# A 16-float tile between two buffers: x, gh and gl 64 bytes further up in SBUF

## The chip, the cores and the metric

The kernel runs on one core of a Trainium2 chip. The metric is the device time of one execution in microseconds; for the kernel before it is 677.24 us, the median of three runs (676.77 to 677.29).

## The reference

Attention over 4 batches, 8 heads, 768 positions and head dimension 64, in which a query sees the first 4 keys (sinks) and the last 128, then a two-layer network over the 3072 tokens with a leaky rectifier between the layers:

```python
keep = is_sink | in_window
scores = np.where(keep, scale * (q @ k.T), -1e9)
a = softmax(scores)
x = (a @ v)                      # 3072 tokens x 512
h = x @ w_in                     # 512 -> 2048
g = np.maximum(h, 0.0) + alpha * np.minimum(h, 0.0)
out = (g @ w_out).astype(np.float32)   # 2048 -> 512
```

## The kernel before

The tokens go in 12 chunks of 256 (`NCHUNK`), the 2048 hidden units in 16 blocks of 128 (`NF`). Everything of a chunk is kept in halves: a value is split into a part rounded to the TensorE's fp32r format and the rest, so x is `xh` and `xl`, the hidden activations are `gh` and `gl`, and each weight block `w0` to `w15` holds four rows of 512 floats in each partition: high and low part of w_in, high and low part of w_out.

For a chunk c and a block f there is one **pair** of products. `gemm1` (line 894) makes 12 matmuls of 256 columns: for each of 4 slices of the 512 inputs, high weights with `xh`, high weights with `xl`, low weights with `xh`. The weight slice (128x128) is loaded into the array, `xh` or `xl` streams past it. `gemm2` (lines 931, 932 and 929) makes 6 matmuls of 512 columns with the roles exchanged: a 128x128 half of `gh` or `gl` is loaded into the array, and a row of the weight block streams past. Between the two, ScalarE and VectorE make `g`, `gh` and `gl` out of the PSUM bank (lines 898 to 901). There are 12 x 16 = 192 pairs; gemm2 of a block follows gemm1 of the block two places later (`LAG`).

Attention of the next chunk (scores at lines 597 and 598, softmax at 610 and 614, values at 786 and 875) is fed in between the pairs. The order on each engine comes out of `Plan`, a scheduler that draws a schedule from estimated costs and then ties the instructions of each engine into that order. No address enters its costs.

Two SBUF pools matter here. `const` holds the constants and the 16 weight blocks and lies at the low addresses. `main` lies behind it; its tiles are laid one behind the other in the order of the `several(...)` and `pool.tile(...)` calls, so every tile's address follows from the sizes ahead of it. Worked out from the built program, per partition and modulo 512 bytes:

| tile | start modulo 512, before | role at TensorE |
|---|---|---|
| w0 to w13, w15 | 32 | loaded in gemm1, streamed in gemm2 |
| w14 | 192 | the same |
| xh, xl (2 each) | 224 | streamed in gemm1 |
| gh, gl (3 each) | 224 | loaded in gemm2 |
| kq0, kq1 | 96, 128 | both, in the scores |
| sinkT, vs | 224, 224 | streamed, loaded, in the sinks' product (line 859) |

All slices that one matmul takes of x, gh, gl or a weight block begin a multiple of 512 bytes into the tile, so the remainder modulo 512 is the same for all of them. In gemm1 the streamed operand thus lies 192 bytes beyond the loaded one modulo 512 (32 bytes for block 14); in gemm2 the loaded one lies 192 bytes beyond the streamed one (32 for block 14).

Of the kernel before, what the change touches and what calls it, by code (L numbers as in the profile page):

```python
# [9 lines left out]
F32 = mybir.dt.float32  # L10
# [9 lines left out]
P = 128  # L20
# [301 lines left out]
def program(ctx, tc, qk, pairs, vp, vq, vs, w, par, out):  # L322
# [3 lines left out]
    pool = fast.enter_context(tc.tile_pool(name="main", bufs=1))  # L326
# [8 lines left out]
    def several(name, n, shape, dtype):  # L335
        plan.kind(name, [pool.tile(shape, dtype, name=f"{name}{i}") for i in range(n)])
# [17 lines left out]
    several("sinkT", 1, [P, QC], F32R)  # L354
    several("vs", 1, [P, DM], F32R)
    several("ob", 2, [P, DM], F32)
    several("xh", 2, [P, KT, QC], F32R)
    several("xl", 2, [P, KT, QC], F32R)
    several("g", 2, [P, QC], F32)
# [918 lines left out]
```

## Time and profile before

| what | us |
|---|---|
| median of the runs shown | 677.24 |
| runs shown | 676.77, 677.24, 677.29 |
| span of the profiled execution, first to last instruction | 676.2 |
| median less that span: what lies around it | 1.0 |
| VectorE busy in the span | 525.8 |
| ScalarE busy in the span | 397.5 |

The profile comes from one execution, of which the page gives the span and no other time. Matmuls are pipelined: the record of one reaches over the start of the next, so the distance from start to start, not the length of the records, says what a matmul costs in a stream.

### The profile page before, as it was taken

What the parts mean: (1) busy time and instruction counts of PE and PEld (TensorE: products, weight loads), DVE (VectorE), ACT (ScalarE), POOL (GpSimd) and SP (SyncE); (2) the same over time, 40 slices, a digit from 0 to 9 for tenths busy, and PEclk for the clock granted to TensorE, in tenths of its full rate; (3) what the DMA queues carried; (4) which work ended last, traced back from release to release, by engine and by line L of the source; (5) the groups of instructions that cost most, each with busy time, mean ns of one, the idle gap of its engine ahead of it and who ended that gap; (6) DMA issues with size and microseconds to landing.
All of it is one profiled execution on the core that took longest, in us unless ns stands there. A gap on an engine that the chain in (4) does not pass through costs nothing.

```text
span 676.2 us, 13243 instructions
## 1 busy us (share of the span) xinstructions
PE 663.8 (98%) x4532; PEld 580.5 (86%) x4534; DVE 525.8 (78%) x1750; ACT 397.5 (59%) x1066; POOL 34.5 (5%) x115
## 2 busy tenths in 40 slices
PE   9989999999999999999999999999999999999996
PEld 4577898888989989989988988988998988998995
DVE  6999999968967976986986995995895994994331
ACT  6989888827636726736636735644744753853332
POOL 2110000001000000000000000010000000000000
PEclk9979999999999999999999999999999999999999
DMA  8684641424343453443443433552542543420001
GB/s 314 229 277 151 241 187 39 127 71 147 122 133 107 122 148 93 145 132 95 141 118 114 143 107 93 163 140 61 172 128 78 161 128 88 142 94 17 32 2 35
DMA packets 58683, 85.19 MB, mean 126 GB/s; under 512 B 9072, under 2 KB 35056, under 8 KB 58608
## 3 DMA queue, kind: packets, MB, share of 16 engines
q1 hardware_dynamic: 55056, 71.17, 34.7%
q10 hardware_dynamic: 3552, 13.11, 5.4%
q8 instruction: 37, 0.61, 0.4%
q14 instruction: 38, 0.31, 0.1%
HBM read 67.22 MB, written 17.04 MB: 125 GB/s over the span
## 4 chain that ended last, share of the span: by engine, by line
PE 83%; DVE 9%; ACT 5%; issue 2%; POOL 0%; DMA 0%; ACTq 0%; SPq 0%; POOLq 0%
PE bank L894 35%; PE bank L931 12%; PE bank L932 11%; PE bank L929 11%; PE bank L786 3%; PE bank L598 3%; PE bank L597 3%; PE bank L875 2%; DVE wa L396 2%; ACT pt L614 1%; ACT wa L382 1%; DVE wa L394 1%; DVE w L404 1%; DVE g L899 1%; DVE gl L901 1%
## 5 line engine op out<-in xcount | busy, mean ns | idle before, releaser
L894 PE MATMUL bank<-xh,w 128*128 128x256 f32 x1536 | 307.9, 283 | 0.4 <-DVE g L899 0.2
L894 PEld LDWEIGHTS bank<-xh,w 128*128 128x128 f32 x1536 | 250.6, 189 | 9.0 <-DVE g L899 3.0
L894 PE MATMUL bank<-xl,w 128*128 128x256 f32 x768 | 215.1, 280 | 0.1
L898 ACT ACTIVATE g<-bank,param 128x256 f32<-128x256 f32 x192 | 90.5, 472 | 117.4 <-PE bank L894 113.1
L931 PE MATMUL bank<-w,gh 128*128 128x512 f32 x382 | 151.7, 397 | 0.2 <-ACT gh L900 0.2
L932 PE MATMUL bank<-w,gh 128*128 128x512 f32 x382 | 150.1, 393 | 0.0
L894 PEld LDWEIGHTS bank<-xl,w 128*128 128x128 f32 x768 | 145.2, 189 | 4.4 <-DVE xl L808 0.3
L614 ACT ACTIVATE pt<-pt,nm 128x260 f32<-128x260 f32 (+1 forms) x192 | 94.5, 493 | 53.5 <-DVE nm L610 53.1
L899 DVE TENSOR_TENSOR g<-bank,g 128x256 f32<-128x256 f32 x192 | 79.7, 419 | 51.4 <-ACT g L898 50.9
L929 PE MATMUL bank<-w,gl 128*128 128x512 f32 x382 | 119.5, 394 | 0.0
L900 ACT CAST gh<-g 128x256 fp32r<-128x256 f32 x192 | 76.9, 404 | 59.7 <-DVE g L899 59.6
L901 DVE TENSOR_TENSOR gl<-g,gh 128x256 fp32r<-128x256 f32 x192 | 80.5, 423 | 26.5 <-ACT gh L900 23.0
L610 DVE CUSTOM_DVE_ANT_0 pt<-bank,masks 128x260 f32<-128x260 f32 (+1 forms) x192 | 75.0, 401 | 19.3 <-PE bank L598 15.5
L929 PEld LDWEIGHTS bank<-w,gl 128*128 128x128 f32 x382 | 70.7, 188 | 16.2 <-issue 0.7
L931 PEld LDWEIGHTS bank<-w,gh 128*128 128x128 f32 x382 | 71.9, 188 | 9.5 <-ACT gh L900 0.7
L932 PEld LDWEIGHTS bank<-w,gh 128*128 128x128 f32 x382 | 71.9, 188 | 8.3
L563 DVE TENSOR_TENSOR kq<-stage,kq 64x392 fp32r<-64x392 f32 x80 | 45.3, 566 | 2.7
L659 POOL TENSOR_TENSOR sink<-pt,ri 128x8 f32<-128x8 f32 x80 | 20.8, 264 | 504.7 <-DVE ri L644 358.8
L597 PE MATMUL bank<-kq 128*128 128x260 f32 (+1 forms) x160 | 44.4, 278 | 1.3 <-DVE nm L610 1.3
L598 PE MATMUL bank<-kq 128*128 128x260 f32 (+1 forms) x160 | 45.0, 281 | 0.0
L655 DVE CUSTOM_DVE_ANT_0 comb<-pt,ri 128x128 f32<-128x128 f32 x136 | 43.1, 343 | 0.4
L561 ACT CAST kq<-stage 128x392 fp32r<-128x392 f32 x80 | 40.9, 512 | 0.7 <-ACT pt L614 0.2
(130 smaller groups left out, 686.9 us busy)
## 6 DMA issues: line engine op xcount, KB each, us to landing
stage<-qk SPq DMA_DIRECT2D x80, 324.0 KB, 2.9
wraw<-w ACTq DMA_DIRECT2D x12, 1024.0 KB, 5.9
swap<-comb SPq DMA_DIRECT2D x36, 256.0 KB, 2.0
comb<-swap SPq DMA_DIRECT2D x36, 256.0 KB, 3.2
v<-vq SPq DMA_DIRECT2D x36, 192.0 KB, 2.5
out_dram<-ob SPq DMA_DIRECT2D x22, 256.0 KB, 3.5
wraw<-w SPq DMA_DIRECT2D x4, 1024.0 KB, 12.0
v<-vp SPq DMA_DIRECT2D x8, 192.0 KB, 6.9
```

What stands on the lines that cost most here:

```text
L597: nc.tensor.matmul(s[:, w0], qh()[:, qs], ks()[:, kw], start=True, stop=False)
L598: nc.tensor.matmul(s[:, w0], ql()[:, qs], ks()[:, kw], start=False, stop=True)
L610: op("DVE", dve(n), lambda: nc.vector.tensor_tensor_reduce(out=pt.at[:, u, w0], in0=s.at[:, w0], in1=masks[:, i, w0], scale=-0.125, scalar ...
L614: op("ACT", exp(n), lambda: nc.scalar.activation(pt.at[:, u, w0], pt.at[:, u, w0], AF.Exp, bias=nm.at[:, h, u:u + 1], scale=-1.0, accum_ou ...
L894: nc.tensor.matmul(h(), fin.at[:, 0, part, ks], rhs.at[:, kt], start=(kt == 0 and n == 0), stop=(kt == KT - 1 and n == 2))
L898: op("ACT", act(QC, True), lambda: nc.scalar.activation(g.at, h(), AF.Copy, scale=alt[:, f:f + 1]), reads=[bk, known("param")], writes=[g])
L899: op("DVE", dve(QC), lambda: nc.vector.tensor_tensor(g.at, h(), g.at, ALU.max), reads=[bk], writes=[g])
L900: op("ACT", cast(QC), lambda: nc.scalar.copy(gh.at, g.at), reads=[g], writes=[gh])
L901: op("DVE", dve(QC), lambda: nc.vector.tensor_tensor(gl.at, g.at, gh.at.bitcast(F32), ALU.subtract), reads=[g, gh], writes=[gl])
L929: nc.tensor.matmul(o2[j].at, gl.at[:, js], fin.at[:, 1, 0], start=False, stop=(f == NF - 1))
L931: nc.tensor.matmul(o2[j].at, gh.at[:, js], fin.at[:, 1, 0], start=(f == 0), stop=False)
L932: nc.tensor.matmul(o2[j].at, gh.at[:, js], fin.at[:, 1, 1], start=False, stop=False)
```

## The change

One tile of 16 floats (64 bytes in each partition) is asked of the pool `main` behind `ob` and ahead of `xh`. Nothing writes or reads it.

```diff
     several("vs", 1, [P, DM], F32R)
     several("ob", 2, [P, DM], F32)
+    pool.tile([P, 16], F32, name="between")
     several("xh", 2, [P, KT, QC], F32R)
     several("xl", 2, [P, KT, QC], F32R)
     several("g", 2, [P, QC], F32)
     several("gh", LAG + 1, [P, QC], F32R)
     several("gl", LAG + 1, [P, QC], F32R)
```

Every tile of `main` behind it moves up by 64 bytes: xh, xl, g, gh, gl from 224 to 288 modulo 512, and the small tiles pf, wrap, masks and tri with them. All tiles ahead of it and all of `const` stay. The instructions of every engine, their order, their waits and their shapes are the same in both programs; only these addresses differ. In gemm1 the streamed x now lies 256 bytes beyond the loaded weights modulo 512 (96 for block 14), and in gemm2 the loaded gh and gl lie 256 beyond the streamed weights (96 for block 14).

## The prediction

> **What bounds the kernel now.** I read the page's busy times and clock first, then busy times by stretch, then who waited, and last the starts of single matmuls in the timeline.
>
> ```profile
> span 676.2 us, 13243 instructions
> PE 663.8 (98%) x4532; PEld 580.5 (86%) x4534; DVE 525.8 (78%) x1750; ACT 397.5 (59%) x1066; POOL 34.5 (5%) x115
> PEclk9979999999999999999999999999999999999999
> ...
> 28.00:100.00 72.00, 69.09 (x452) 57.86 (x451) 69.62 (x128) 62.31 (x131) 4.00 (x8) 0.95 0.62 214
> 100.00:300.00 200.00, 198.40 (x1361) 176.72 (x1359) 167.19 (x594) 119.75 (x337) 11.57 (x34) 1.00 0.38 114
> 300.00:600.00 300.00, 299.82 (x2107) 269.85 (x2107) 237.83 (x867) 170.31 (x489) 12.96 (x48) 1.00 0.41 121
> ...
> PE bank L588 <- DVE nm L610: 1.7, 2, 1.2
> PE bank L597 <- DVE nm L610: 1.3, 3, 0.8
> ```
>
> TensorE is busy 98% of the span at a granted clock of nine tenths or more in 39 of 40 slices, and its longest waits on another engine sum to 1.7 and 1.3 us. From 100 to 600 us it is busy 498.2 of 500 us, with VectorE at 405: a nanosecond taken off or put on a matmul there shows at the end almost whole. From 28 to 100 us VectorE is as full (69.62 of 72 us), so a faster TensorE would gain little there.
>
> The work that the change touches is nearly all of TensorE's:
>
> ```profile
> L894 PE MATMUL bank<-xh,w 128*128 128x256 f32 x1536 | 307.9, 283 | 0.4 <-DVE g L899 0.2
> L894 PE MATMUL bank<-xl,w 128*128 128x256 f32 x768 | 215.1, 280 | 0.1
> ...
> L931 PE MATMUL bank<-w,gh 128*128 128x512 f32 x382 | 151.7, 397 | 0.2 <-ACT gh L900 0.2
> L932 PE MATMUL bank<-w,gh 128*128 128x512 f32 x382 | 150.1, 393 | 0.0
> ...
> L929 PE MATMUL bank<-w,gl 128*128 128x512 f32 x382 | 119.5, 394 | 0.0
> ```
>
> 1536 + 768 = 2304 matmuls of gemm1 are 192 groups of 12. The means of 283 and 394 ns are lengths of overlapping records; what counts is start to start. The last chunk has no attention beside it, so it shows the pairs bare. Its rows for the first matmul of gemm2 of successive blocks, and of gemm1 where I need it (start in us, length, line):
>
> ```profile
> 627.18 0.40 PE L931 MATMUL bank<-w,gh 128*128 128x512 f32 x1
> ...
> 641.00 0.39 PE L931 MATMUL bank<-w,gh 128*128 128x512 f32 x1
> ...
> 642.37 0.28 PE L894 MATMUL bank<-xh,w 128*128 128x256 f32 x1
> ...
> 643.76 0.39 PE L931 MATMUL bank<-w,gh 128*128 128x512 f32 x1
> ...
> 645.14 0.27 PE L1048 MATMUL bank<-ident,worst 128*1 128x128 f32 x1
> ...
> 646.66 0.40 PE L931 MATMUL bank<-w,gh 128*128 128x512 f32 x1
> ...
> 663.50 0.40 PE L931 MATMUL bank<-w,gh 128*128 128x512 f32 x1
> ...
> 666.27 0.39 PE L931 MATMUL bank<-w,gh 128*128 128x512 f32 x1
> ...
> 667.64 0.40 PE L931 MATMUL bank<-w,gh 128*128 128x512 f32 x1
> ...
> 669.05 0.39 PE L916 MATMUL bank<-w,gh 128*128 128x512 f32 x1
> ```
>
> The rows name no block; by the program's order 643.76 starts block 5 of this chunk, 663.50 block 12, and 666.27, 667.64 and 669.05 blocks 13, 14 and 15. From 627.18 to 643.76 are six pairs: (643.76 - 627.18) / 6 = 2.763 us each. Then one small transpose (line 1048) slips in, and from 646.66 to 663.50 the next six take 16.84 / 6 = 2.807 us each. Same instructions, same clock, nothing waited for: **the same pair has a fast and a slow repeating pattern**, and a disturbance of a few tenths of a microsecond flips one into the other. The loads of the next weights run beside the streaming of the present ones all the while, so what differs can only be how those two reads, and the other engines' accesses, fall together. That is the quantity that an address can move.
>
> **The change part by part.** It adds no instruction, takes none, moves none past another and adds no wait; a tile that nothing touches costs nothing. What changes is the distance between the two SBUF reads of a matmul, modulo 512: 192 to 256 in gemm1, and 320 to 256 (counted from the loaded to the streamed operand) in gemm2. The distance counts modulo 512 or a divisor of it: the slices of a block lie 512 or 1024 bytes apart, and I find no step along them. Four readings price what a distance does.
>
> *Block 14* lies elsewhere, so it is the trace's own experiment: its distances are 32 in gemm1 and 480 in gemm2. Its gemm2 runs from 667.64 to 669.05, 1.41 us; block 13's just before ran from 666.27 to 667.64, 1.37 us. So nearness of the two operands costs 0.04 us per gemm2 here, or 3%. An address does count.
>
> *Distance 0* is shown by the sinks' product, whose operands both lie at 224, with 256 columns as in gemm1:
>
> ```profile
> 400.23 0.64 PE L859 MATMUL bank<-sinkT,vs 128*128 128x256 f32 x4
> 400.71 0.28 PE L894 MATMUL bank<-xh,w 128*128 128x256 f32 x1
> ```
>
> Four in 0.48 us are 0.120 us each, against (643.76 - 642.37) / 12 = 0.116 us in gemm1 at distance 192.
>
> *The best stretch of gemm1* lies in the second half of that fast group:
>
> ```profile
> 642.97 0.39 PE L894 MATMUL bank<-xh,w 128*128 128x256 f32 x2
> ...
> 643.65 0.28 PE L894 MATMUL bank<-xh,w 128*128 128x256 f32 x1
> ```
>
> With the 643.76 row, seven matmuls in 0.79 us: 0.113 us each. A gemm1 that ran so throughout would take 1.354 us.
>
> *A stream without such operands* is the warm-up on a two-element tile, 512 columns of bf16:
>
> ```profile
> 11.08 1.25 PE L1086 MATMUL bank<-idle 128*128 128x512 bf16 x5
> ```
>
> ```profile
> 14.03 0.38 PE L1086 MATMUL bank<-idle 128*128 128x512 bf16 x1
> ```
>
> One of them alone lasts 0.38 us, so of the 1.25 us of five four steps take 0.87, 0.218 each, and six would take 1.305 us where gemm2 takes 1.37 to 1.41.
>
> [...]
>
> **The sum.** The two patterns of the last chunk hold six pairs each; I take that mix, 2.785 us, for the kernel. Distances 32 or 0 are dearer than 192 by the rows above, and 256 is as far apart as two operands can lie modulo 512; both products get it at once. I take from this that the fast pattern holds more of the time. With all pairs in it the gain is 0.022 us per pair. How many pairs pass it on:
>
> ```profile
> 28.00:100.00 72.00, 31.26 (x222) 29.54 (x222) 0.95 0.62 214
> ```
>
> That row is of line 894 alone: 222 of its matmuls, 18.5 pairs, start where VectorE is full. I count them as worth nothing; 192 - 18.5 = 173.5 pairs give 173.5 x 0.022 = 3.8 us. The profiled span goes from 676.2 to 672.4; with the 1.0 us around it, 673.4 against the median of 677.24, or -0.56%. The other edits at nothing: `g`, `masks` and `tri` are VectorE and ScalarE operands, and those engines are off the path in the stretches above; if the 64 bytes slowed them, the 28 to 100 us stretch, which holds no slack, would show it first. Bounds of the unknown: below, the best stretch of gemm1 with a gemm2 at block 13's price, 1.354 + 1.37 = 2.724 us, 173.5 x 0.061 = 10.6 us less, 666.6; above, distance 0's price in gemm1 and block 14's in gemm2, 12 x 0.120 + 1.41 = 2.85 us, 192 x 0.065 = 12.5 us more, 689.7. The value taken is nearest to the rows of the same instructions at the same distances, which is why I prefer it to the far ends.
>
> **The rivals.**
>
> *No change, 677.2.* For it: the shift is a whole 64 bytes. If the reads meet by position within 64 bytes, or 256 lies in a flat part between 192 and 320, nothing moves. The two distances in use now lie either side of 256, and block 14 differs from the others by 160 bytes, not a multiple of 64, so its price may be one of alignment and not of distance. Against: the flip by one transpose shows that small things choose the pattern, so an exact standstill needs the reads to be wholly alike. [...]
>
> *Slower, the slow pattern everywhere.* The choice of pattern hangs on where in the pair the reads of the next weights meet the stream; at 256 the meeting lies at another place, and it may be one that settles in the slow pattern, as after the transpose at 645.14. Price 192 x 0.022 = 4.2 us, 681.4; it decides if more than about two pairs in three repeat in 2.81 us. For it: no row shows a matmul at distance 256, and slow is where the trace ends up after a disturbance. Worse still, at distance 0's price, 689.7.
>
> *Faster by more*, the meetings gone from gemm1: 666.6, as worked out above. For it the seven matmuls at 0.113; against it that they stand only at a group's end, when VectorE and ScalarE have finished.
>
> That the change does not do what it says is excluded by the addresses of the built program.
>
> **How the numbers follow.** The fast pattern, 673.4 (own range 671.5 to 675.5): 0.34. Much faster, near 666.6: 0.07. No change: 0.33. Slow pattern, near 681.4: 0.18. Distance 0's price, near 689.7: 0.08. A measurement of this kernel can tell about 0.2% (1.4 us) from no change; so faster 0.41, same 0.33, slower 0.26. The range reaches from 667.0 to 683.0: it leaves out the dearest case and half of the cheapest, with a little of the slow one, and takes in the rest.
>
> **What would show it.** In the profile after, the last chunk's pairs, read from one line-931 row to the same of the next block: 2.76 after the transpose too if the forecast holds, 2.76 and 2.81 as now if nothing changes, 2.81 from the chunk's start if slow. Block 14, now at distance 96, is read by its gemm2: below 1.41 us if distance is the cause. The records of VectorE and ScalarE should keep their means; if they change, my account is wrong in kind. It would be wrong in size if gemm2 and gemm1 go opposite ways, since I let both gain.

## The result, and the profile after

| kernel | median us | runs | span of the profiled execution |
|---|---|---|---|
| before | 677.00 | 4 runs, 676.73 to 677.29 | 676.2 |
| after | 682.28 | 4 runs, 682.03 to 683.70 | 680.0 |

The change makes the kernel slower: ratio 1.0078, 95% interval 1.0063 to 1.0093, or 5.3 us. 673.4 was forecast, on the other side; the time lies near the top of the range of 667.0 to 683.0.

The two profiled executions ran at different granted clocks, 0.994 before and 0.999 after. In every run of this case whose span is on record, the time is 1.9 to 2.1 us above the span. The profile of before therefore belongs to an execution of about 678.2 us, and the 1.0 us that the table of before puts around the span mixes two executions. Runs of before at a clock of 0.998 have spans of 674.5 to 674.9; the span of after lies 5 us above those, as the medians do.

The page of the kernel after, all line numbers up by one: span, TensorE's busy time, the granted clock, the chain that ended last by engine and by line, and three of the costliest groups.

```profile
span 680.0 us, 13245 instructions
...
PE 667.9 (98%) x4534; PEld 585.4 (86%) x4534; DVE 525.9 (77%) x1750; ACT 399.1 (59%) x1066; POOL 35.0 (5%) x115
...
PEclk9999999999999999999999999999999999999999
...
PE 89%; DVE 5%; ACT 4%; issue 1%; POOL 0%; ACTq 0%; POOLq 0%
...
L895 PE MATMUL bank<-xh,w 128*128 128x256 f32 x1536 | 313.3, 285 | 0.3 <-DVE g L900 0.2
...
L895 PE MATMUL bank<-xl,w 128*128 128x256 f32 x768 | 216.8, 282 | 0.1
...
L902 DVE TENSOR_TENSOR gl<-g,gh 128x256 fp32r<-128x256 f32 x192 | 80.3, 422 | 26.6 <-ACT gh L901 22.9
```

TensorE's busy time grew by 4.1 us, the span by 3.8. The groups of gemm1 (now line 895) grew. VectorE's `gl` took 422 ns each; before, it took 423:

```profile
L901 DVE TENSOR_TENSOR gl<-g,gh 128x256 fp32r<-128x256 f32 x192 | 80.5, 423 | 26.5 <-ACT gh L900 23.0
```

VectorE's busy time stood still (525.8 and 525.9 us). ScalarE's grew by 1.6 us, but its operation on each bank of gemm1 took 474 ns against 472, and it waited longer for that bank (121.3 us against 113.1), so it follows TensorE. TensorE's clock was no lower (the profiled execution of before even had one slice at seven tenths). Its waits on other engines sum to 5.3 us after and 5.5 before. The three longest of the kernel after (total us, times, longest):

```profile
PE bank L589 <- DVE nm L611: 2.2, 2, 1.1
PE bank L1087 <- DVE fm L545: 1.0, 1, 1.0
PE bank L598 <- DVE nm L611: 0.9, 2, 0.8
```

So the time is in the spacing of the matmuls themselves. The last chunk again, from the timeline of after: the first matmul of gemm2 of the last block of the chunk before it and, six pairs later, of block 5; the small transpose; then blocks 6 and 12.

```profile
630.43 0.40 PE L932 MATMUL bank<-w,gh 128*128 128x512 f32 x1
...
647.35 0.40 PE L932 MATMUL bank<-w,gh 128*128 128x512 f32 x1
...
648.74 0.27 PE L1049 MATMUL bank<-ident,worst 128*1 128x128 f32 x1
...
650.27 0.40 PE L932 MATMUL bank<-w,gh 128*128 128x512 f32 x1
...
667.20 0.40 PE L932 MATMUL bank<-w,gh 128*128 128x512 f32 x1
```

(647.35 - 630.43) / 6 = 2.820 us per pair ahead of the transpose and (667.20 - 650.27) / 6 = 2.822 behind it, against 2.763 and 2.807 before. Here the pair takes the same time on both sides of the transpose, more than in either pattern of before. Inside it, gemm1 of block 10 from the same timeline:

```profile
654.48 0.28 PE L895 MATMUL bank<-xh,w 128*128 128x256 f32 x1
654.60 0.28 PE L895 MATMUL bank<-xl,w 128*128 128x256 f32 x1
...
655.79 0.28 PE L895 MATMUL bank<-xh,w 128*128 128x256 f32 x1
655.91 0.40 PE L932 MATMUL bank<-w,gh 128*128 128x512 f32 x1
```

From the second matmul to the first of gemm2 are eleven steps in 1.31 us by these rounded rows, 0.119 each; by the starts in ns each of them is 120 ns.

For the comparisons below I take, from the starts in each timeline, every gemm1 whose twelve matmuls and every gemm2 whose six follow one another with nothing between and without a gap (no step from start to start above 0.14 us in gemm1 or 0.26 in gemm2), from its first start to the start of whatever comes next. Block 14 is left out. I average over these groups, 132 or 133 of gemm1 and 158 or 162 of gemm2 in each run. Before: gemm1 1.393 us, gemm2 1.386. After: 1.430 and 1.381. As an estimate for all 192 pairs that is 192 x (0.037 - 0.005) = +6.1 us, of which 5.3 us show in the medians.

### The profile page after: what moved, and what is told of

The parts are those of the page before. It is cut to its first block, busy times and chain, and to the rows that moved or that the text cites. A ratio compares the mean times of both kernels' runs of the same rounds, so it can differ in the third digit from the quotient of the medians.

```text
span 680.0 us, 13245 instructions
## 1 busy us (share of the span) xinstructions
PE 667.9 (98%) x4534; PEld 585.4 (86%) x4534; DVE 525.9 (77%) x1750; ACT 399.1 (59%) x1066; POOL 35.0 (5%) x115
## 4 chain that ended last, share of the span: by engine, by line
PE 89%; DVE 5%; ACT 4%; issue 1%; POOL 0%; ACTq 0%; POOLq 0%
PE bank L895 39%; PE bank L933 12%; PE bank L932 12%; PE bank L930 12%; PE bank L787 3%; PE bank L599 3%; PE bank L598 3%; PE bank L876 2%; ACT pt L615 1%; PE bank L1087 1%; DVE wa L397 1%; ACT wa L383 1%; PE bank L860 1%; DVE pt L611 1%; DVE w L405 1%
## 5 line engine op out<-in xcount | busy, mean ns | idle before, releaser
L895 PE MATMUL bank<-xh,w 128*128 128x256 f32 x1536 | 313.3, 285 | 0.3 <-DVE g L900 0.2
L899 ACT ACTIVATE g<-bank,param 128x256 f32<-128x256 f32 x192 | 91.0, 474 | 122.8 <-PE bank L895 121.3
```

The costliest lines, as they stand in the source:

```text
L895: nc.tensor.matmul(h(), fin.at[:, 0, part, ks], rhs.at[:, kt], start=(kt == 0 and n == 0), stop=(kt == KT - 1 and n == 2))
L899: op("ACT", act(QC, True), lambda: nc.scalar.activation(g.at, h(), AF.Copy, scale=alt[:, f:f + 1]), reads=[bk, known("param")], writes=[g])
```

## The experiments

Theory A: the cost of a matmul goes with how far its two SBUF operands lie apart, modulo some power of two. Theory B: the position of x, of gh or of one of the small tiles behind them matters by itself. Theory C: any disturbance deals the repeating pattern anew, and the loss is luck. The experiments change addresses only: instructions, order and waits are the same in all the programs, and each computes the whole of the reference. Ratios are to the kernel before in the same set of runs.

**Which tiles, and against what.** Only x moved:

```diff
+    pool.tile([P, 16], F32, name="between")
     several("xh", 2, [P, KT, QC], F32R)
     several("xl", 2, [P, KT, QC], F32R)
+    pool.tile([P, 112], F32, name="behind")
     several("g", 2, [P, QC], F32)
```

> Only xh and xl move by 64 bytes (224 to 288 modulo 512); g, gh, gl and the small tiles behind them move by a whole 512 and keep their remainder 224. Distance theory (what a matmul costs is set by how far its streamed operand lies beyond the loaded one modulo 512): gemm1 takes 0.120 us per matmul in a row as after the change, gemm2 stays at 1.37 to 1.40 us; time 682 to 684 us. If the loss comes from gh, gl, g, masks or tri: 677 us. If the pattern is dealt anew by any disturbance: somewhere from 674 to 682 us, with pairs of both kinds.

Measured: 683.28 us, ratio 1.0075 (1.0057 to 1.0093); gemm1 1.433 us, gemm2 1.385. The whole loss is there, with gh, gl and the small tiles at their old remainders.

Only g, gh, gl and what follows moved:

```diff
     several("xl", 2, [P, KT, QC], F32R)
+    pool.tile([P, 16], F32, name="behind")
     several("g", 2, [P, QC], F32)
```

> Only g, gh, gl and the small tiles behind them move by 64 bytes; xh and xl stay. Distance theory: gemm1 stays at 113 and 118 ns per matmul, gemm2 as after the change, a few ns shorter in the mean; 676 to 677 us. If the loss comes from gh, gl, g, masks or tri: 682 us.

Measured: 676.84 us, ratio 0.9989 (0.9979 to 1.0000). Gemm2 fell to 1.373 us, and gemm1, untouched, came out at 1.404: 94 of its 132 groups took 1.405 us or more, where 58 did before. So the mean of a product also depends on what the other product does to the mix of the patterns. Its timeline, gemm2 of one block and the gemm1 behind it:

```profile
654.42 0.39 PE L932 MATMUL bank<-w,gh 128*128 128x512 f32 x1
...
655.78 0.28 PE L895 MATMUL bank<-xh,w 128*128 128x256 f32 x1
...
657.20 0.39 PE L932 MATMUL bank<-w,gh 128*128 128x512 f32 x1
```

1.36 us for gemm2, where the kernel before had 1.374 at the least, and 1.42 for gemm1. What one product gained the other gave back, and the interval touches no change: moving gh and gl is worth about a tenth of a per cent here, and two at the most.

Weights and everything behind them moved alike:

```diff
     size = const.tile([P, NF], F32, name="size")
+    const.tile([P, 16], F32, name="ahead")
     sizes = held(size)
```

> A tile of 64 bytes at the head of the constants moves the weights and everything behind them by 64 bytes alike: x, gh and gl lie at 288 modulo 512 as after the change, the weights at 96, and every distance is that of before. Distance theory: 677 us, gemm1 with 113 and 118 ns per matmul. If the position of x itself decides: 682 us, 120 ns per matmul.

Measured: 677.42 us, ratio 0.9996 (0.9985 to 1.0007); gemm1 1.393 us, gemm2 1.386, as before to a nanosecond. x lies at 288 modulo 512 here too, exactly as after the change, and costs nothing: B falls for x's own position. The two patterns stand as before; block 6 to block 12 behind the transpose, where (664.20 - 647.36) / 6 = 2.807:

```profile
647.36 0.40 PE L932 MATMUL bank<-w,gh 128*128 128x512 f32 x1
...
664.20 0.40 PE L932 MATMUL bank<-w,gh 128*128 128x512 f32 x1
```

The counterpart moves the weights and leaves the tiles of the main pool at their remainders:

```diff
     size = const.tile([P, NF], F32, name="size")
+    const.tile([P, 112], F32, name="ahead")
...
+    pool.tile([P, 16], F32, name="between")
     several("stage", 2, [P, QC + KC], F32)
```

> x, gh, gl and all other tiles of the main pool keep their remainder modulo 512; the constants with the weights move up by 448 bytes, so the weights lie at 480 and x lies 256 beyond them, as after the change but with the weights moved in its place. Distance theory (streamed against loaded operand, period 256): 682 to 683 us, gemm1 at 0.120 us per matmul. If x against other tiles of its own pool, or its own position, made the loss: 677 us.

Measured: 683.12 us, ratio 1.0083 (1.0064 to 1.0102); gemm1 1.433 us. The loss appears without x moving against any tile of its own pool, so it is x against the weights. (The weights' own position is no better reading: they lie at 32 before and after the change alike, and at 96 at no cost.) Blocks 6 to 12 of the last chunk, (668.44 - 651.51) / 6 = 2.822 us as after the change:

```profile
651.51 0.40 PE L933 MATMUL bank<-w,gh 128*128 128x512 f32 x1
...
668.44 0.40 PE L933 MATMUL bank<-w,gh 128*128 128x512 f32 x1
```

**The period.** The tile `between` was made 512, 256 and 320 bytes long. For 512 bytes:

```diff
-    pool.tile([P, 16], F32, name="between")
+    pool.tile([P, 128], F32, name="between")
```

> x, g, gh, gl and the tiles behind them move up by 512 bytes, so every remainder modulo 512 is that of before. If 512 bytes is a period of the effect: 677 us and the same two patterns of 2.76 and 2.81 us per pair in the last chunk. If the distance counts beyond 512: another time, up to 682 us. If any move deals the pattern anew: 674 to 682 us.

Measured: 678.40 us, ratio 1.0007 (0.9997 to 1.0017); gemm1 1.394, gemm2 1.386. Any move dealing the pattern anew (C) would hardly give the same two means. With 64 floats, 256 bytes:

> 256 bytes up: distance 448. Narrow place at 256: gemm1 0.116 us, 677 us. If the cost falls with the distance from some best place: no more than a guess, 0.113 to 0.122 us per matmul, 671 to 688 us.

Measured in one run: 677.23 us beside 678.65 before (the same run of before stands beside those with 320, 32 and 128 bytes; at a clock of 0.994 it lies some 1.3 us above the medians of before, so the means of the groups are the better evidence); gemm1 1.394, gemm2 1.385. Moving by 256 bytes changes nothing. With 80 floats, 320 bytes:

> 320 bytes up: distance 0, as the sinks' product has it, whose four matmuls took 0.120 us each before. If the distance alone decides: gemm1 0.120 us, 682 to 684 us. If the sinks' price came from their own place: 0.113 to 0.118 us, 673 to 678 us.

Measured in one run: 682.76 us beside 678.65; gemm1 1.430, gemm2 1.381: to the nanosecond the numbers of the changed kernel, at a remainder 256 bytes away from it. Its blocks 6 to 12, (667.76 - 650.83) / 6 = 2.822:

```profile
650.83 0.40 PE L932 MATMUL bank<-w,gh 128*128 128x512 f32 x1
...
667.76 0.40 PE L932 MATMUL bank<-w,gh 128*128 128x512 f32 x1
```

So the pattern repeats with 256 bytes, not 512, and the change put the two operands **at distance 0**. Half of that, 128, is no period: below, gemm1 takes 1.405 us at 64 and 1.389 at 192 in one and the same run.

**The places between.** These kernels have `between` with 8, 32 and 48 floats (32, 128 and 192 bytes):

> x, gh, gl 32 bytes up: distance 224 modulo 512 in both products, halfway between before and after. Theory of a graded cost (it rises from 192 to 256): gemm1 between 0.116 and 0.119 us per matmul, time 678 to 681 us. Theory of a narrow place at 256: as before, 677 us. Theory of alignment (only multiples of 64 are alike): something else than both, up to 0.123 us per matmul.

Measured in one run: 681.62 us beside 678.65; gemm1 1.418 (0.118 per matmul), gemm2 1.394. So the cost is not confined to a narrow place at 256: 32 bytes short of it gemm1 is already dearer than at 192.

> 128 bytes up: distance 320. Narrow place at 256: gemm1 at 0.116 us per matmul as at 192, 677 us. If everything beyond 256 is dear: 0.119 us or more, 682 us or more. Gemm2, which has its operands the other way round: 1.37 to 1.40 us.

Measured in one run: 683.75 us beside 678.65; gemm1 1.406, gemm2 1.398. A narrow place at 256 fell here too: gemm1 is dearer than at 192 and gemm2 dearer than anywhere else with one distance for all.

> 192 bytes up: distance 384, which is 128 modulo 256, the one multiple of 64 not seen so far. Period 256: a price of its own, between those of 64 (gemm1 1.406 us per group of 12) and 192 (1.393 us), 677 to 681 us. Period 128 would make it 0 once more: 1.430 us and 682 us.

Measured: 683.34 us, ratio 1.0086 (1.0068 to 1.0105); gemm1 1.432, gemm2 1.389. Half a period away, gemm1 is as dear as at 0. The price between that was expected did not come.

Two attempts at a better place put x 16 bytes to either side of 192, with gh and gl at 0 as in the run that moved them alone. Each x tile begins 4 floats into a longer one, with fillers that keep all four alike modulo 256. The first kernel (the second has 56 floats more ahead of them, and 16 behind):

```diff
-    several("xh", 2, [P, KT, QC], F32R)
-    several("xl", 2, [P, KT, QC], F32R)
+    for name in ("xh", "xl"):
+        views = []
+        for i in range(2):
+            t = pool.tile([P, KT * QC + 4], F32R, name=f"{name}{i}")
+            views.append(t[:, 4:].rearrange("p (k x) -> p k x", k=KT))
...
+        plan.kind(name, views)
+    pool.tile([P, 8], F32, name="behind")
```

> x 208 bytes beyond the weights modulo 256 and gh, gl at 0 (the best seen for each: gemm1 at 192, gemm2 at 0). If gemm1's price falls further on this side of 192: below 1.393 us per group, with gemm2 at 1.373 down to 672 us. If it climbs towards 224 (1.418 us): about 679 us.

> x 176 bytes beyond the weights modulo 256, gh and gl at 0. If gemm1's price falls on this side of 192: below 1.393 us per group and down to 672 us. If it climbs towards 160 (1.422 us, from block 14 with everything 128 bytes up): about 679 us.

Measured: 682.75 us, ratio 1.0084 (1.0062 to 1.0106), and 682.38 us, ratio 1.0067 (1.0048 to 1.0087); gemm1 1.428 us in both. Both hopes missed. The run to hold these against is the one that moved gh and gl alone (gemm1 1.404 us, 676.84 us in all). Both readings are even dearer than the next places further out, 1.422 us at 160 (block 14 in the run 128 bytes up, four groups) and 1.418 at 224. So 192 is a dip between 160 and 224, and the kernel before stood in it. How narrow it is stays open: in these two runs alone x begins at an odd multiple of 16 bytes, and no run separates such an alignment from the distance.

By distance of the streamed x beyond the weights, modulo 256 (gh and gl lie at the same distance unless the table says otherwise):

| distance | run | gemm1, us | gemm2, us | time, us |
|---|---|---|---|---|
| 0 | after | 1.430 | 1.381 | 682.28 |
| 0 | weights moved back | 1.433 | 1.387 | 683.12 |
| 0 | 320 bytes up | 1.430 | 1.381 | 682.76, one run |
| 0 | x alone | 1.433 | 1.385 (gh, gl at 192) | 683.28 |
| 64 | 128 bytes up | 1.406 | 1.398 | 683.75, one run |
| 128 | 192 bytes up | 1.432 | 1.389 | 683.34 |
| 176 | x alone, 16 bytes less | 1.428 | 1.384 (gh, gl at 0) | 682.38 |
| 192 | before | 1.393 | 1.386 | 677.00 |
| 192 | all moved by 64 | 1.393 | 1.386 | 677.42 |
| 192 | gh, gl alone | 1.404 | 1.373 (gh, gl at 0) | 676.84 |
| 208 | x alone, 16 bytes more | 1.428 | 1.388 (gh, gl at 0) | 682.75 |
| 224 | 32 bytes up | 1.418 | 1.394 | 681.62, one run |

**Local or common; which two reads.** Two more runs. In the first the weight blocks lie 64 bytes further apart, so one run has all four distances:

```diff
-            fin.at = const.tile([P, 2, 2, DM], F32R, tag=f"w{f}", name=f"w{f}")
+            t = const.tile([P, 4 * DM + 16], F32R, tag=f"w{f}", name=f"w{f}")
+            fin.at = t[:, :4 * DM].rearrange("p (i h x) -> p i h x", i=2, h=2)
```

> The weight blocks lie 64 bytes further apart, so that x lies 0 beyond blocks 4, 8, 12, 13, 64 beyond 0, 3, 7, 11, 128 beyond 2, 6, 10, 15, and 192 beyond 1, 5, 9 modulo 256 (32 beyond 14), in one run. If the distance of x to the weights of the block decides: groups of 12 of 1.43 us in the first and the third, 1.39 to 1.41 us in the second and the fourth. If it is something that was common to each earlier run: all blocks alike.

Measured in one run: 681.26 us beside 677.73. Averaged over all chunks by distance, gemm1 took 1.428 at 0, 1.405 at 64, 1.429 at 128 and 1.389 at 192. The last chunk, gemm1 of blocks 9 (distance 192), 10 (128), 11 (64) and 12 (0), each from its first row to the next row:

```profile
650.89 0.28 PE L895 MATMUL bank<-xh,w 128*128 128x256 f32 x1
...
652.31 0.40 PE L932 MATMUL bank<-w,gh 128*128 128x512 f32 x1
...
653.71 0.28 PE L895 MATMUL bank<-xh,w 128*128 128x256 f32 x1
...
655.14 0.40 PE L932 MATMUL bank<-w,gh 128*128 128x512 f32 x1
...
656.51 0.28 PE L895 MATMUL bank<-xh,w 128*128 128x256 f32 x1
...
657.92 0.40 PE L932 MATMUL bank<-w,gh 128*128 128x512 f32 x1
...
659.32 0.28 PE L895 MATMUL bank<-xh,w 128*128 128x256 f32 x1
...
660.76 0.39 PE L932 MATMUL bank<-w,gh 128*128 128x512 f32 x1
```

1.42, 1.43, 1.41 and 1.44 us: block by block, not by run. Block 9 shows the dearer of 192's two patterns here; over the whole run half of its kind took 1.371 or less. The averages by distance, near those of the whole runs with one distance each, show that the distance of the block at hand sets the cost; the four rows alone would not.

In the second only xl moved, so that one stream in three lies at 256:

```diff
+    pool.tile([P, 16], F32, name="between")
     several("xl", 2, [P, KT, QC], F32R)
+    pool.tile([P, 48], F32, name="behind")
     several("g", 2, [P, QC], F32)
```

> Only xl moves by 64 bytes; xh stays at 192 beyond the weights, xl is at 256; gh, gl keep their remainder modulo 256. In a group the matmuls go high weights with xh, high weights with xl, low weights with xh. If the stream meets the load of the next matmul's weights: 4 of 12 streams are at the dear distance, gemm1 about a third of the way from 1.393 to 1.430 us, near 1.405 us, and the step that is longer is always the same one of three. If only the common pattern of all twelve counts: all or nothing, 677 or 682 us.

Measured in one run: 680.32 us beside 677.73; gemm1 1.415 us, over half of the way from 1.393 to 1.430 and not the third that single streams would give, yet not all or nothing either. Of the steps from the fourth on, those that begin with xh and high weights and those with xl took 118.7 ns in the mean, the third kind 116.4. Neither expectation holds, so which two reads meet, a stream with the load of the next weights beside it or with its own, **stays open**. So does why the cost has this shape over the distance.

## Why the prediction was wrong

**What bounds the kernel** held: all that changed was the spacing of TensorE's matmuls, and it came through to the end (about 6.1 us in the pairs, 5.3 in the time). That an address could move that spacing, and that it would act in gemm1 and gemm2 by the distance between the operands, held too (only x moved, all moved alike, weights moved back).

**The step that failed** is the sentence "256 is as far apart as two operands can lie modulo 512". The part on the change had said that the distance counts modulo 512 "or a divisor of it", and the sum then went by 512 alone. The period is 256: moving by 256 gave gemm1 1.394 and gemm2 1.385 us, as before, and moving by 320 gave those of after. At that period 256 is distance 0, which the prediction had priced: the sinks' product, 0.120 us per matmul of 256 columns. After the change gemm1 runs at 120 ns per step. The right row was quoted, but its case was placed at 689.7, beyond the upper end of the range, with a chance of 0.08. That the time still fell inside the range is luck: what reached that far up was the price of another case, the slow pattern.

**Nearness as the cause** was a second fault in the same step. Block 14's gemm2 was read as the price of lying near (32 against 192), 0.04 us from one pair of readings; over all chunks it is 1.406 against 1.386, 0.02. The sweep shows no such rule: gemm1 is 1.430 at 0, 1.406 at 64, 1.432 at 128 and 1.393 at 192, and in block 14, at 32, it takes 1.402. Two readings, one each for near and far, could not tell a steady rise from a curve that goes up and down.

**The two patterns.** The term of the sum, 0.022 us per pair for going wholly to the fast pattern, had no counterpart: at distance 0 the last chunk shows no second pattern, since a pair takes 2.820 us ahead of the transpose and 2.822 behind it. The rival on the slow side was near in time (681.4) but not in mechanism: gemm1 did not settle in the old slow pattern of 2.807 but in a dearer one. That the patterns come from how the reads of the next weights and of the stream fall together was the author's conjecture, in the forecast and in this rival alike; no trace or run shows it. The rival at distance 0's price had the right price for gemm1, and was too dear (689.7) because it added block 14's gemm2 at 1.41 us, which does not come with distance 0: gemm2 there is 1.381.

**Gemm2** went the way forecast, by 5 ns a group, and the prediction named the case in which the products go opposite ways as the one that would break its size. Block 14's gemm2, now at distance 96, fell from 1.406 to 1.388 us as foretold, but the reason given for it, distance, does not stand, since its gemm1 rose from 1.402 to 1.430.

**No change** was refuted: the same instructions take 0.8% longer at another address. Gemm1 takes 1.393 or 1.430 us by the distance of its two operands. The span of the profile grew by 3.8 us and the median by 5.3 because the profiled execution of before ran at the lower clock of the two (0.994 against 0.999).

## What to carry to other kernels

Where a matmul loop is bound by TensorE (98% busy here), the addresses of the streamed and the loaded operand can be a tuning parameter. Here it was worth about 3% of one of the two products (gemm1 1.393 to 1.433 us) and 0.8% of the kernel. Sweep it by small fillers, and read start-to-start distances, not record lengths (0.28 us each in gemm1 here, at steps of 0.12). Before reasoning from a remainder, find the period: one kernel moved by half of the supposed period would have shown it. An arrangement that nobody chose can already be as good as any that is tried: no placement tried here beats the kernel before by more than its measurement can tell (0.9989, 0.9979 to 1.0000, at the best).

## What the runs showed of the hardware that was not expected

- The spacing of gemm1's matmuls (256 columns, fp32r, 128x128 weights) depends on the distance of the two SBUF operands modulo 256 bytes, with 113 or 118 ns at 192 and 120 ns at 0.
- With gh and gl at 0, x 16 bytes off 192 costs gemm1 24 ns a group (1.404 us at 192, 1.428 at 176 and at 208) and the kernel 0.8% (676.84 us against 682.38 and 682.75). Whether it is the distance or the alignment to 16 bytes is not separated.
- At 192 two patterns of one instruction sequence, 2.763 and 2.807 us a pair, each repeat for six blocks of the last chunk, the first ahead of one small transpose and the second behind it; at distance 0 a pair takes the same on both sides of it (2.820 and 2.822 us).
